# First FFN of an attention and two-FFN kernel: the next batch's scores ahead of its first two weight sets, and split sets and fetches in the first batch

## The chip, the cores and the metric

One core of a Trainium2 chip runs the whole kernel. Its engines are TensorE (PE in the profile, with PEld for the loading of weights), VectorE (DVE), ScalarE (ACT), GpSimd (POOL) and SyncE (SP). The metric is the device time of one execution in microseconds (us); lower is better. SP, ACT and POOL also issue transfers; the core's 16 DMA engines carry them out, and the profile shows the transfers of SP as queue q1, those of POOL as q0 and those of ACT as q10.

## The reference

```python
def _attn_ref(x, state):                      # x (8, 8, 512, 64), state (8, 8, 32, 64)
    scores = scale * np.matmul(x, state.transpose(0, 1, 3, 2))
    a = softmax(scores)
    xread = np.matmul(a, state)
    scores2 = scale * np.matmul(state, x.transpose(0, 1, 3, 2))
    a2 = softmax(scores2)
    sread = np.matmul(a2, x)
    return np.concatenate([xread, sread], axis=2)

def _moe_ref(x, w1, w2, w3, w_out):           # 4608 tokens, 512 -> 1024 -> 1024 -> 512
    h = (x @ w1) * (x @ w2) @ w3
    return h @ w_out

def _moe2_ref(x, w_gate, w_val, w_out):       # 512 -> 1536 -> 512
    return (sigmoid(x @ w_gate) * (x @ w_val)) @ w_out
```

`softmax` stands here for the lines that subtract the maximum, take the exponential and divide by the sum. The three stages run one after the other on the 4608 rows of the attention.

## The kernel before, in words

The kernel never forms the attention's `xread` for the first FFN. Since `xread @ w1` is `a @ (state @ w1)`, it makes for each of the 8 batches the small products of `state` with `w1` and `w2` and uses these as the weights of that batch. They come in four **sets** (quarters of the FFN's width). `StateWeights.fetch(q)` loads 1 MB of the converted `w1` and `w2` into one of two buffers `wq`; `StateWeights.make(q)` multiplies `state` with it on PE (results `psw`, two banks a set), and ACT and DVE split each bank into a high and a low part (`sw`). A `wq` buffer is free for the next fetch once PE has read it. So of the four fetches a batch needs, the third (quarter 2) can only be issued when `make(0)` is through PE, and the fourth when `make(1)` is.

The first FFN runs batch by batch (`t` from 0 to 7 in the loop at the end of the listing). In a batch `ffn1` has 12 places where other work is hung in, the **slots**: before each of the eight products `pab` (slots 0 to 7, `JF` is 8) and before each of the four output blocks `py` (slots 8 to 11). In these slots the kernel makes ready the next batch: `xt` in slots 6 and 7 turns its x (`pxt` to `xT`), `scores` and what follows in slot 8 computes both score products (`psc`) and the first half of the softmax, slot 9 the second half, slot 10 or 11 the sets 2 and 3. For `t` of 1 to 6 slot 8 held, in this order, `sread` (`psr`, the last reader of this batch's x), a piece of the conversion of the second FFN's weights (`todo`, which ends in stores `wd` and `wod` on POOL), `make(0, 1)`, the scores, and `get(2, 3)`, which fetches the quarters 2 and 3. In batch 0 everything is one slot later, and its sets 2 and 3 are in slot 11.

`load_x` loads the x of the batch after the next in eight transfers `xn` of 128 KB, one a head, each in rows of 64 numbers (256 bytes). Its buffer is free when `sread` has read the old x, so the eight wait for `psr`.

In this part of the kernel only PE's order is written out by hand. The order on ACT, DVE, POOL and SP is worked out at build time by the framework, from its own estimate of when an instruction could start, and is then fixed: an engine that waits for one instruction does not go on to the next.

Of the kernel before, what the change touches and what calls it, by code (L numbers as in the profile page):

```python
# [127 lines left out]
def tile_state_attention__then__gated_ffns(  # L128
# [31 lines left out]
    JF = DFF // P  # L160
# [112 lines left out]
    with tc.manual_schedule(engines={mybir.EngineType.PE}):  # L273
# [7 lines left out]
        def load_x(b):  # L281
            t = at.tile([P, G, SC, 2, D], F32, name="xn", bufs=2)
            xn[b] = t
            for h in range(H):
                nc.sync.dma_start(
                    out=t[:, h // 2, :, h % 2], in_=x[b, h].rearrange("(p c) d -> p c d", c=SC)
                )
# [236 lines left out]
        def behind(fn):  # L524
            with tc.issue_after(last["raw"].ins):
                fn()
# [470 lines left out]
        nxt = StateWeights(order[1])  # L997
# [76 lines left out]
        def open_wst():  # L1074
            p2["wst"] = tc.alloc_tile_pool(name="wst", bufs=1, reuse_waits="tile")
# [8 lines left out]
        def in_place(fn):  # L1084

            with tc.issue_after(p2["act"].ins), tc.issue_after(p2["dve"].ins):
                fn()
# [100 lines left out]
        for t, b in enumerate(order):  # L1188
            if t:
                cur, nxt = nxt, StateWeights(order[t + 1]) if t + 1 < B else DirectWeights()  # L1190
            slots = {i: [] for i in range(JF + KM)}
            if t == 0:
                slots[JF] += [after_wp, sreadt]
                after = {}
            for i, fns in after.items():
                slots[i] += fns
            if t == 1:
                open_wst()
            if t:
                for i in range(t == 1, JF + KM):  # L1200
                    if todo:
                        slots[i].append(lambda fn=todo.pop(0): in_place(fn))
            if t + 1 < B:
                go = lambda t=t: load_x(order[t + 1])
                if t:
                    slots[0].append((lambda go=go: behind(go)) if t < 2 else go)
                before, after = attention(order[t + 1])[:2] if t else (before1, after1)

                def get(*qs, nxt=nxt):
                    for q in qs:  # L1210
                        nxt.fetch(q)

                if t == 0:
                    slots[JF + 1].append(lambda nxt=nxt: nxt.make(0, 1))
                    slots[JF + 1].append(lambda get=get: get(2, 3))
                    for i, fns in before.items():
                        if i >= JF:
                            slots[i + 1] += fns
                    slots[JF + 3].append(lambda nxt=nxt: nxt.make(2, 3))
                else:  # L1220
                    slots[0].append(lambda get=get: get(0, 1))
                    for i, fns in before.items():
                        slots[i] += fns
                    slots[JF].insert(2, lambda nxt=nxt: nxt.make(0, 1))
                    slots[JF].append(lambda get=get: get(2, 3))
                    slots[JF + 2].append(lambda nxt=nxt: nxt.make(2, 3))
            else:
                slots[JF + 2].append(lambda nxt=nxt: nxt.weights(0))
            if t + 1 == B:
                slots[JF + 3].append(open_c1)  # L1230
            ffn1(t, S, 2, cur.weights, aT[b], slots, u0 if t == 0 else None)
# [3 lines left out]
        slots = {i: [] for i in range(JF + KM)}  # L1235
# [475 lines left out]
```

## Time and profile before

| | |
|---|---|
| median of 3 runs | 1285.46 us (1285.43 to 1286.4) |
| the profiled execution | 1287.98 us |
| its span, first to last instruction | 1286.2 us |
| PE busy | 1267.1 us, 99% of the span |
| DVE busy | 957.4 us, 74% |
| ACT busy | 669.1 us, 52% |
| granted TensorE clock | 0.998 of full speed |
| first FFN, batches 1 to 6 | from 132.0 to 448.5 us of the span |

The profile is of one execution, whose time lies 2.5 us above the median of the plain runs; sums made from its rows are differences, and are set on the median.

### The profile page before, as it was taken

Reading aid. Unit: us, or ns where it says so; the run is one execution under the profiler, and the core shown is the slowest. Engines: PE = TensorE matmul, PEld = TensorE weight load, DVE = VectorE, ACT = ScalarE, POOL = GpSimd, SP = SyncE. Lnnn points to the kernel's source line nnn. Section 1 sums busy time; section 2 is a strip of 40 time slices with the busy share of each in tenths; the row PEclk is TensorE's granted clock in tenths of the full one; section 3 lists DMA queues with packets and bytes.
Section 4 is the critical chain, followed back from the end, with each engine's and each line's share of the span. In section 5 each row is a group of like instructions: output and inputs, shape, how many; then the busy total and the mean of one; then the engine's idle time right before and its main releaser. Section 6 shows DMA issues by size and latency. Waiting matters only on the chain.

```text
span 1286.2 us, 21643 instructions
## 1 busy us (share of the span) xinstructions
PE 1267.1 (99%) x7868; PEld 1107.4 (86%) x7868; DVE 957.4 (74%) x1848; ACT 669.1 (52%) x1308; POOL 86.6 (7%) x162
## 2 busy tenths in 40 slices
PE   9999999999999999999999999999999999999996
PEld 8777877878878789988887888889999999999996
DVE  8996779788797856175959657687686868687666
ACT  8994757757677556352444343362345344434432
POOL 0000000000000000000000500004000300021000
PEclk9999999999999999999999999999999999999999
DMA  9886697896978722587765867668888888878853
GB/s 345 265 263 241 210 331 264 286 307 236 330 261 298 273 112 75 190 270 221 230 202 175 259 203 241 195 194 271 276 291 262 267 274 292 259 254 277 255 178 99
DMA packets 169121, 312.86 MB, mean 243 GB/s; under 512 B 45368, under 2 KB 63288, under 8 KB 162104
## 3 DMA queue, kind: packets, MB, share of 16 engines
q1 hardware_dynamic: 153492, 257.21, 62.3%
q0 software_dynamic: 9344, 44.57, 9.5%
q10 hardware_dynamic: 6180, 9.70, 2.2%
q8 instruction: 63, 1.03, 0.3%
q14 instruction: 42, 0.34, 0.1%
HBM read 256.38 MB, written 55.05 MB: 242 GB/s over the span
## 4 chain that ended last, share of the span: by engine, by line
PE 81%; DVE 9%; ACT 5%; DMA 3%; issue 1%; SPq 0%; ACTq 0%; POOL 0%; DVEq 0%; POOLq 0%
PE psA L1438 20%; PE po L1608 16%; PE psB L1438 10%; PE pab L235 9%; PE py L235 8%; PE pab L238 5%; PE psC L1438 4%; PE py L238 4%; DMA wq<-w12d 2%; PE psw L543 2%; DVE y L1168 1%; ACT r L207 1%; DVE p L1474 1%; DVE ph L1168 1%; PE pxt L300 1%
## 5 line engine op out<-in xcount | busy, mean ns | idle before, releaser
L1438 PE MATMUL psA<-y,wt 128*128 128x384 f32 (+1 forms) x1440 | 299.8, 356 | 0.0
L1438 PEld LDWEIGHTS psA<-y,wt 128*128 128x128 f32 x1440 | 259.0, 188 | 22.5
L1608 PE MATMUL po<-ph,wo 128*128 128x384 f32 (+1 forms) x1260 | 251.7, 358 | 5.7 <-ACT sv L168 3.3
L1608 PEld LDWEIGHTS po<-ph,wo 128*128 128x128 f32 x1260 | 225.1, 188 | 29.6 <-ACT sv L168 6.3
L168 ACT ACTIVATE u<-psA 128x384 f32<-128x384 f32 (+1 forms) x120 | 64.0, 533 | 228.0 <-PE psA L1438 213.7
L1438 PE MATMUL psB<-y,wt 128*128 128x384 f32 (+1 forms) x720 | 159.5, 356 | 0.0
L1438 PEld LDWEIGHTS psB<-y,wt 128*128 128x128 f32 x720 | 130.0, 188 | 11.2
L235 PE MATMUL pab<-aT,sw 128*128 128x512 f32 x512 | 139.4, 394 | 0.0
L235 PE MATMUL py<-u,wp 128*128 128x512 f32 (+1 forms) x576 | 131.9, 381 | 0.0
L235 PEld LDWEIGHTS py<-u,wp 128*128 128x128 f32 x576 | 102.8, 188 | 28.2 <-issue 8.3
L235 PEld LDWEIGHTS pab<-aT,sw 128*128 128x128 f32 x512 | 94.4, 188 | 19.2 <-DVE s L356 0.4
L1560 DVE TENSOR_TENSOR acc<-po,acc 128x384 f32<-128x384 f32 (+1 forms) x140 | 82.8, 605 | 31.3 <-PE po L1608 30.9
L1532 POOL DMA_DIRECT2D out<-sv x112 | 61.7, 551 | 600.1 <-DVE sv L1527 595.5
L1465 DVE TENSOR_TENSOR p<-psB,u 128x384 f32<-128x384 f32 (+1 forms) x60 | 36.6, 610 | 81.7 <-ACT u L168 68.9
L1467 ACT ACTIVATE p<-p 128x384 f32<-128x384 f32 (+1 forms) x90 | 50.7, 563 | 83.1 <-DVE p L1465 83.1
L1438 PE MATMUL psC<-y,wt 128*128 128x384 f32 (+1 forms) x360 | 79.8, 356 | 0.0
L238 PE MATMUL pab<-aT,sw 128*128 128x512 f32 x256 | 78.9, 390 | 0.0
L1168 DVE TENSOR_TENSOR ph<-p,ph 128x384 fp32r<-128x384 f32 (+1 forms) x120 | 70.2, 605 | 7.4 <-ACT ph L168 6.4
L1438 PEld LDWEIGHTS psC<-y,wt 128*128 128x128 f32 x360 | 65.0, 188 | 5.6
L238 PE MATMUL py<-u,wp 128*128 128x512 f32 (+1 forms) x288 | 67.7, 377 | 0.0
L168 ACT ACTIVATE ph<-p 128x384 fp32r<-128x384 f32 (+1 forms) x120 | 63.5, 564 | 0.2 <-DVE p L1168 0.2
L168 ACT ACTIVATE ph<-t 128x384 fp32r<-128x384 f32 (+1 forms) x90 | 49.4, 564 | 26.4 <-DVE t L1168 26.1
(142 smaller groups left out, 1836.6 us busy)
## 6 DMA issues: line engine op xcount, KB each, us to landing
wt<-wd SPq DMA_DIRECT2D x420, 256.0 KB, 3.5
wo<-wod SPq DMA_DIRECT2D x105, 512.0 KB, 3.7
wq<-w12d SPq DMA_DIRECT2D x32, 1024.0 KB, 8.7
raw<-in_moe_w SPq DMA_DIRECT2D x32, 512.0 KB, 6.8
wd<-wstb POOLq DMA_DIRECT2D x12, 1024.0 KB, 5.4
raw<-in_moe_w_out SPq DMA_DIRECT2D x20, 512.0 KB, 6.4
wd<-wsta POOLq DMA_DIRECT2D x12, 768.0 KB, 4.3
xn<-in_x SPq DMA_DIRECT2D x56, 128.0 KB, 7.1
```

Source lines behind the costliest of these rows:

```text
L168: return nc.scalar.activation(out=o, in_=i, func=AF.Copy)
L207: lambda: nc.scalar.activation(out=r16[:, :, 0], in_=lo, func=AF.Copy, scale=2.0**-29),
L235: nc.tensor.matmul(o, w[i], xx[k], start=begin and n == 0 and i + k == 0, stop=False)
L238: nc.tensor.matmul(o, w[1 - late], xx[late], start=False, stop=end and n == len(pairs) - 1)
L543: nc.tensor.matmul(pts[k][NS * g : NS * g + NS, a * WQ : (a + 1) * WQ], stT[64 * k : 64 * k + 64, g, self.b * NS : (self.b + 1) * NS], w[6 ...
L1168: nc.vector.tensor_tensor(out=o, in0=x0, in1=x1, op=ALU.subtract)
L1438: nc.tensor.matmul(o, w[:, i, kb * P : (kb + 1) * P], xx[kb][h], start=start, stop=i == 1 and kb == 1, skip_group_check=True,)
L1465: nc.vector.tensor_tensor(out=t, in0=o, in1=kept[a, what], op=ALU.add)
L1467: later(2, 0.0, lambda: nc.scalar.activation(out=t, in_=t, func=AF.Sigmoid))
L1532: nc.gpsimd.dma_start(out=dst[:, :, i * P : (i + 1) * P], in_=t[32 * i : 32 * i + 32].rearrange("t j d e -> t j (d e)"),)
L1560: nc.vector.tensor_tensor(out=acc[d, cc], in0=o, in1=acc[d, cc], op=ALU.add)
L1608: nc.tensor.matmul(o, w[:, jj, i, d * P : (d + 1) * P], x[h], start=k in (1, 6, 2) and jj == 0 and i + h == 0, stop=jj == 1 and i == 1, sk ...
```

## The change

For `t` of 1 to 6, `make(0, 1)` moves behind the scores in slot 8. In batch 0 the sets 0 and 1 are taken apart: `make(0)` and the fetch of quarter 2 stay in slot 9 ahead of the scores, `make(1)` and the fetch of quarter 3 go to slot 10.

```diff
                 if t == 0:
-                    slots[JF + 1].append(lambda nxt=nxt: nxt.make(0, 1))
-                    slots[JF + 1].append(lambda get=get: get(2, 3))
+                    slots[JF + 1].append(lambda nxt=nxt: nxt.make(0))
+                    slots[JF + 1].append(lambda get=get: get(2))
+                    slots[JF + 2].insert(0, lambda nxt=nxt: nxt.make(1))
+                    slots[JF + 2].insert(1, lambda get=get: get(3))
                     for i, fns in before.items():
                         if i >= JF:
                             slots[i + 1] += fns
@@ -1221,7 +1223,7 @@
                     slots[0].append(lambda get=get: get(0, 1))
                     for i, fns in before.items():
                         slots[i] += fns
-                    slots[JF].insert(2, lambda nxt=nxt: nxt.make(0, 1))
+                    slots[JF].append(lambda nxt=nxt: nxt.make(0, 1))
                     slots[JF].append(lambda get=get: get(2, 3))
                     slots[JF + 2].append(lambda nxt=nxt: nxt.make(2, 3))
```

On SP, in batch 1 (the same in batches 2 to 5), these are the transfers around slot 8; `w12d_59` and `w12d_60` are the quarters 2 and 3 of this batch, `xn` the loads of the x two batches on. Lines with - are the order before, with + the order after.

```order
 L181 DMA raw<-in_moe_w_gate 128x4x256 x2
 L181 DMA raw<-in_moe_w_val 128x4x256
-L285 DMA xn<-in_x 128x4x64 x3
+L285 DMA xn<-in_x 128x4x64 x5
 L519 DMA wq<-w12d_59 128x2048
 L519 DMA wq<-w12d_60 128x2048
-L285 DMA xn<-in_x 128x4x64 x5
+L285 DMA xn<-in_x 128x4x64 x3
 L181 DMA raw<-in_moe_w_val 128x4x256
```

Two of the eight `xn` loads have moved from behind the two fetches to ahead of them, although the diff names neither. Batch 6 has no `xn` loads.

On ACT, at the same place of batch 1, these are the evictions of the sets (`sw`), the exponentials of the scores (`e`, `st`), the eviction of the first output block (`ysb`) and, two rows on, its store; the numbers in names only tell instances apart.

```order
 L168 ACTIVATE u_1953<-asb 128x512
-L451 ACTIVATE sr<-psr,r_1498 128x64 x2
-L168 ACTIVATE sw_2017<-psw 128x512 x2
-L168 ACTIVATE sw_2041<-psw 128x512 x2
-L348 ACTIVATE e_2048,s_2050<-psc,m_2049 128x512 x2
+L451 ACTIVATE sr<-psr,r_1472 128x64 x2
+L168 ACTIVATE sw_2046<-psw 128x512 x2
+L348 ACTIVATE e_2000,s_2002<-psc,m_2001 128x512 x2
+L168 ACTIVATE sw_2070<-psw 128x512 x2
 L373 ACTIVATE st<-st 128x1024
 L168 ACTIVATE ysb<-py 128x512
```

The second set's evictions went behind the two exponentials; DVE's order changes likewise.

On PE, in batch 0, these are the two places where sets are made in slots 9 and 10, each behind a block `py`.

```order
 L238 MATMUL py<-u_1401,wp_81 128x512
 L238 MATMUL py<-u_1385,wp_81 128x512
-L543 MATMUL psw<-wq,stT 32x256 x32
+L543 MATMUL psw<-wq,stT 32x256 x16
 L323 MATMUL psc<-xT,stT 32x512 x8
 L235 MATMUL py<-u_1205,wp_80 128x512
@@ -326,4 +326,5 @@
 L238 MATMUL py<-u_1401,wp_81 128x512
 L238 MATMUL py<-u_1385,wp_81 128x512
+L543 MATMUL psw<-wq,stT 32x256 x16
 L235 MATMUL py<-u_1205,wp_80 128x512
 L235 MATMUL py<-u_1206,wp_80 128x512
```

Half of the 32 matmuls moved one output block on. In batches 1 to 6 PE's only difference is that `psw` and `psc` have changed places in slot 8.

## Rows read from the trace of the kernel before

**Rows 1.** The page: span, and PE's busy time, share and instructions.

```profile
span 1286.2 us, 21643 instructions
PE 1267.1 (99%) x7868; PEld 1107.4 (86%) x7868; DVE 957.4 (74%) x1848; ACT 669.1 (52%) x1308; POOL 86.6 (7%) x162
```

**Rows 2.** Windows of batches 1 to 5: length, busy time of engines, clock, DMA share.

```profile
132.02:185.03 53.01, 52.76 (x426) 42.03 (x425) 43.17 (x84) 35.49 (x67) 2.85 (x5) 1.00 0.77 267
185.03:238.05 53.02, 52.80 (x427) 42.09 (x426) 44.56 (x86) 36.28 (x69) 3.38 (x6) 1.00 0.79 269
238.05:290.80 52.75, 52.75 (x427) 42.11 (x426) 44.38 (x86) 36.31 (x69) 3.37 (x6) 1.00 0.87 301
290.80:343.50 52.70, 52.70 (x426) 42.01 (x426) 44.51 (x86) 36.29 (x69) 3.37 (x6) 1.00 0.81 281
343.50:396.00 52.50, 52.50 (x427) 42.10 (x426) 44.40 (x86) 36.56 (x69) 3.38 (x6) 1.00 0.84 288
```

**Rows 3.** Timeline of PE, batch 0, slot 9: start, length, work, idle time before it.

```profile
109.58 1.09 PE L543 MATMUL psw<-wq,stT 64*32 64x256 f32 x32
111.53 1.10 PE L543 MATMUL psw<-wq,stT 64*32 64x256 f32 x32 [0.85 <-DMA wq<-w12d]
112.42 1.07 PE L323 MATMUL psc<-xT,stT 64*32 64x512 f32 x16
113.41 3.92 PE L235 MATMUL py<-u,wp 128*128 128x512 f32 x16
118.99 3.79 PE L235 MATMUL py<-u,wp 128*128 128x512 f32 x16
```

**Rows 4.** Timeline of PE, batch 1: slot 8, then sets 2 and 3.

```profile
156.61 1.10 PE L438 MATMUL psr<-xn,a 128*32 128x64 f32 x64
157.64 1.96 PE L543 MATMUL psw<-wq,stT 64*32 64x256 f32 x64
...
171.60 1.09 PE L543 MATMUL psw<-wq,stT 64*32 64x256 f32 x32
172.95 1.10 PE L543 MATMUL psw<-wq,stT 64*32 64x256 f32 x32 [0.25 <-DMA wq<-w12d]
```

**Rows 5.** Timeline of SP's queue in batch 1.

```profile
157.77 3.09 SPq L285 DMA_DIRECT2D xn<-in_x  x3
160.96 2.29 SPq L519 DMA_DIRECT2D wq<-w12d  x2
163.30 9.25 SPq L285 DMA_DIRECT2D xn<-in_x  x5
```

**Rows 6.** Tile wq, SP's issues from 156 to 165 us and their landing.

```profile
L519 SPq DMA_DIRECT2D wq<-w12d x2: 632/1124/1617, 161.0 to 161.6; - x2
DMA to landing us min/median/max: 9.2/10.2/11.2
```

**Rows 7.** DMA from 166 to 170 us: packets, bytes, share of the engines.

```profile
DMA packets 249, 1.67 MB, mean 418 GB/s; under 512 B 47, under 2 KB 47, under 8 KB 47
q1 hardware_dynamic: 248, 1.65, 100.8%
```

**Rows 8.** DMA from 171 to 172 us.

```profile
DMA packets 913, 0.27 MB, mean 267 GB/s; under 512 B 904, under 2 KB 904, under 8 KB 909
q1 hardware_dynamic: 908, 0.26, 122.3%
```

**Rows 9.** DMA from 172 to 173 us, queue q10.

```profile
q10 hardware_dynamic: 113, 0.22, 67.7%
```

**Rows 10.** Timelines of DVE and ACT, batch 1, around the scores.

```profile
159.81 2.49 DVE L173 TENSOR_TENSOR sw<-psw,sw 128x512 fp32r<-128x512 f32 x4
...
167.18 1.06 ACT L373 ACTIVATE st<-st 128x1024 f32<-128x1024 f32 x1 [0.36 <-DVE st L370]
168.14 0.58 ACT L168 ACTIVATE ysb<-py 128x512 f32<-128x512 f32 x1
...
168.75 0.33 ACTq L1050 DMA_DIRECT2D yd<-ysb  x1
```

**Rows 11.** Batch 5: PE at sets 2 and 3; issue and landing of their fetches.

```profile
382.92 1.96 PE L543 MATMUL psw<-wq,stT 64*32 64x256 f32 x64
...
L519 SPq DMA_DIRECT2D wq<-w12d x2: 723/1002/1282, 372.3 to 373.0; - x2
DMA to landing us min/median/max: 8.7/9.6/10.5
```

**Rows 12.** Tile wq, SP's issues from 105 to 107, then 105 to 127 us: landing.

```profile
DMA to landing us min/median/max: 6.0/6.0/6.0
...
DMA to landing us min/median/max: 5.4/6.0/7.7
```

## The prediction

> **What bounds the kernel now.** The page comes first: PE is busy for 99% of the span [rows 1], so only two things can move the time, work added to PE or a wait of PE. The change adds no matmul and takes none away. It is therefore priced in waits of PE around the slots it touches, and the view for that is PE's timeline, where an idle stretch stands in brackets with its releaser.
>
> The windows by batch show how little there is to win. Batches 1 to 5 do the same work at full clock and take 53.01, 53.02, 52.75, 52.70 and 52.50 us [rows 2]. Taking the shortest as free of waits, the others hold 0.51 + 0.52 + 0.25 + 0.20 = 1.48 us of them. The timeline says where: in batch 1 the matmuls of set 3 wait for their fetch [rows 4]. Sets 2 and 3 would run in 1.89 us as sets 0 and 1 do; set 3 should start 0.95 us behind set 2, at 172.55, and starts at 172.95, so 0.40 of that batch's 0.51 lies here. In batch 5 the 64 matmuls run through without an idle mark [rows 11]. Its later fetch was issued at 373.05 and landed 10.5 us on, at 383.55 [rows 11], while PE wanted it at 382.92 + 0.95 = 383.87: a margin of 0.32 us. So in every one of these batches the fetch of quarter 3 lands just when it is needed, and its landing is what the change has to be asked about. In batch 0 the corresponding wait is for quarter 1, 0.85 us [rows 3].
>
> What sets that landing is seen in three views. SP issues three `xn`, then the two fetches, then five `xn` [rows 5]; the fetches land 9.2 and 11.2 us after issue [rows 6]. From 166 to 170 us queue q1 carries 1.65 MB in 248 packets and fills the engines at 100.8% [rows 7]: that is nearly the whole 2 MB of the two fetches. One microsecond later it carries 908 packets of 256 bytes [rows 8]: the `xn` issued behind them. The queue works its transfers off in the order of issue, and the engines are full, so whatever goes in ahead of the fetches delays them by its own transfer time.
>
> **The change, part by part.**
>
> *Batch 0, make(1) one slot on.* Set 0 runs at 109.58 and takes 0.95 us, the scores 0.99 us [rows 3], and an output block 5.58 us (113.41 to 118.99, [rows 3]). Set 1 then begins at 109.58 + 0.95 + 0.99 + 5.58 = 117.1, and its quarter has landed at 111.5. The wait goes: before, sets 0 and 1 took from 109.58 to 112.42, 2.84 us; without a wait 1.89. Gain 0.95 us. What is late next is quarter 3, fetched only when `make(1)` is through, at about 118.1. PE wants it after another block and set 2, at 118.05 + 5.58 + 0.95 = 124.6. The fetch issued alone at 105.5 landed in 6.0 us [rows 12]; so would this one, at 124.1, and the block covers it with 0.5 us to spare. If it took 7.7, the worst of this stretch [rows 12], 1.2 us would come back. I take nothing, since it too is issued alone.
>
> *Batches 1 to 6, scores ahead of sets 0 and 1.* On PE `psc` (1 us) and `psw` (1.89 us) change places: no time, and `psc` needs only banks and `xT` that are long ready. Quarter 2's buffer comes free 1 us later; SP does not feel it, since it is still issuing `xn` then: before, it reached the fetch at 160.96 [rows 5], 2.4 us after set 0 had run. On DVE the scores no longer stand behind four splits of 2.49 us [rows 10]; by the new order one split still goes before the subtraction and the exponential `st`, so the softmax ends about 1.5 us sooner. Nothing waits for that, it has a whole block of slack; the splits of sets 0 and 1 end later instead, at about 167.5, and PE needs their banks at 171.6. Both cost nothing.
>
> *What the scheduler made of it on SP* decides: in batches 1 to 5 two more `xn` are issued ahead of the fetches of quarters 2 and 3. That is 2 x 128 KB in rows of 256 bytes, 1024 packets. From below: at the 908 packets per us that q1 reached alone [rows 8] they take 1.13 us. From above: if issue and not transfer set the pace, 3.09 us for three [rows 5] makes 2.06 us for two. SP issues the fetches at 160.96 and their data flows from 166 on [rows 5, 7], so issue has some 4 us in hand; I take 1.2, near the transfer's row.
>
> The Trainium skill (DMA: Bandwidth & Descriptors, "Why small descriptors are slow (HBM only)") gives a 256-byte descriptor 11 cycles where 8 carry data. By that the 0.26 MB would take about 0.87 us at [rows 7]'s rate, as an estimate, and the sum below would come to some +4.8 us. The trace has 0.26 MB in a microsecond against 0.41 for large packets [rows 7, 8], a ratio of 0.63 and not 0.73; the row decides.
>
> *A second delay.* The first output block's store `yd` is issued at 168.75, behind `ysb`, which on ACT follows `st` [rows 10]; its packets run from 172 on and take 67.7% of the engines for a microsecond, 0.68 us [rows 9], just after the fetch's data. With `st` 1.5 us sooner the store comes at about 167.3, its packets about 170.5, and the fetch's tail now lasts until about 172: they meet. Between nothing and 0.68 us; I take half, 0.34.
>
> *Sum.* Quarter 3 lands 1.2 + 0.34 = 1.54 us later. Batches 1 to 4 have no margin: 4 x 1.54 = 6.16. Batch 5 has 0.32: 1.22. Batch 6 has no `xn`, nothing. Minus 0.95 in batch 0: **+6.4 us**. The profiled execution's 1287.98 us would become 1294.4. It lies 2.5 us above the median of the runs; on the median, 1285.46 + 6.4 = **1291.9 us**. With both terms at their low ends (1.13, 0): 4 x 1.13 + 0.81 - 0.95 = +4.4; with both high (2.74): 10.96 + 2.42 - 0.95 = +12.4. The likeliest's own range is 1289.9 to 1297.9 us.
>
> **The rivals.**
>
> *The fetches land as before* (not slower). The two `xn` fit into time in which the engines have room, or the landing is set by something else. For it: the later fetch lands only at 161.6 + 11.2 = 172.8 [rows 6], though from 171 on the queue carries hardly anything but small packets [rows 8]; a part of its landing is not transfer. Against it: the full engines of [rows 7]. Then only batch 0 counts: 1285.46 - 0.95 = 1284.5 us. From the first case it parts at a delay d with 4d + (d - 0.32) - 0.95 = 2.57 us, 0.2% of the time and about what a measurement here can tell from no change: d = 0.77 us. If the waits of batches 1 to 4 went too, which needs fetches that land sooner, it would be 1285.46 - 0.95 - 1.48 = 1283.0, still within 0.2%. So "faster" needs a gain that no row shows.
>
> *Issue becomes the bound.* Before, the five `xn` behind the fetches took 9.25 us to issue, 1.85 each [rows 5]: SP was held up. If the fourth and fifth are now held up ahead of the fetches, quarter 3 comes 2.06 us later or more, with the store 2.4: 9.6 + 2.08 - 0.95 = +10.7, 1296.2 us. For it: that row. Against it: after three `xn` and two fetches it was the sixth and later loads that were slow, so the queue takes five.
>
> *Batch 0 loses what it wins*: with a landing of 7.7 us 1.2 of the 0.95 us gained come back, a loss of 0.25, and the first case gives 1293.1 us. I give this 0.1, inside the first case's 0.58.
>
> **How the numbers follow.** First case, a delay above 1.1 us: 0.58. Issue-bound: 0.15. A delay between 0.77 and 1.1 us: 0.07. Less than 0.77, down to none: 0.17. All waits gone: 0.03. Slower by over 0.2% is the first three, 0.80; within 0.2% nearly all the rest; faster I put at 0.03. The range of 1286.0 to 1296.5 leaves out the lowest (no delay at all, 0.12, and all waits gone, 0.03) and the top of the issue-bound case (0.05).
>
> **What the profile after would show.** Right: SP's row reads five `xn`, two fetches, three `xn`; the set-3 matmuls wait some 1.9 us for `wq` in batches 1 to 4 and 1.2 in batch 5; batches 1 to 4 take 54 to 54.5 us; batch 0's wait is gone; batch 6 stays at 52.5. If the waits stand at 2.5 us and the fetches' issue has moved past 164 us in batch 1, issue was the bound. If the `yd` packets lie behind the fetch's data, the second delay was wrong. Prediction wrong: batches 1 to 4 unchanged in length, or a new wait of `py` or `pab` for splits or for `aT`.

## The result, and the profile after

The changed kernel takes 1293.73 us (median of six runs, 1292.94 to 1294.78) against 1285.93 for the kernel before (six runs, 1285.22 to 1287.9): a ratio of 1.0057, 95% interval 1.0046 to 1.0067, which is 5.9 to 8.6 us more (the two medians alone are 7.8 apart). The profiled execution took 1293.67 us, 5.7 more than that of before, with a span 5.5 us longer. The head of its page, beside [rows 1]:

```profile
span 1291.7 us, 21648 instructions
PE 1267.6 (98%) x7868; PEld 1107.5 (86%) x7868; DVE 957.7 (74%) x1848; ACT 669.6 (52%) x1308; POOL 86.6 (7%) x162
```

PE is busy for 0.5 us more than before; the other 5 us are waits. Batches 1 to 6 by windows, with the columns of [rows 2]:

```profile
131.45:185.75 54.30, 52.74 (x426) 42.05 (x425) 43.25 (x84) 35.53 (x67) 2.82 (x5) 1.00 0.76 265
185.75:240.25 54.50, 52.70 (x426) 42.05 (x425) 44.41 (x86) 36.49 (x69) 3.37 (x6) 1.00 0.79 275
240.25:294.32 54.07, 52.70 (x426) 42.05 (x425) 44.49 (x86) 36.38 (x69) 3.36 (x6) 1.00 0.81 278
294.32:348.46 54.14, 52.72 (x426) 42.05 (x425) 44.41 (x86) 36.49 (x69) 3.37 (x6) 1.00 0.80 277
348.46:401.59 53.13, 52.70 (x427) 42.05 (x425) 44.41 (x86) 36.50 (x69) 3.36 (x6) 1.00 0.81 279
401.59:454.05 52.46, 52.46 (x427) 42.16 (x425) 47.05 (x90) 35.89 (x69) 3.86 (x6) 1.00 0.71 266
```

The first five add up to 270.14 us against 263.98 in [rows 2], 6.16 more. The borders in [rows 2] lie up to 0.2 us behind the batches' starts; from `psr` of batch 1 to `psr` of batch 6 it is 263.79 us before and 270.10 after, 6.31 more. Batch 6, the only one of the six without `xn` loads, has no wait at all. PE's timeline of this kernel says where in a batch the time lies (first batch 0, then batches 1, 2, 3 and 5):

```profile
109.71 1.09 PE L543 MATMUL psw<-wq,stT 64*32 64x256 f32 x32
110.60 1.06 PE L323 MATMUL psc<-xT,stT 64*32 64x512 f32 x16
111.59 3.93 PE L235 MATMUL py<-u,wp 128*128 128x512 f32 x16
...
117.27 1.09 PE L543 MATMUL psw<-wq,stT 64*32 64x256 f32 x32
118.29 3.92 PE L235 MATMUL py<-u,wp 128*128 128x512 f32 x16
...
123.95 1.96 PE L543 MATMUL psw<-wq,stT 64*32 64x256 f32 x64
...
156.05 1.10 PE L438 MATMUL psr<-xn,a 128*32 128x64 f32 x64
...
171.04 1.09 PE L543 MATMUL psw<-wq,stT 64*32 64x256 f32 x32
173.69 1.10 PE L543 MATMUL psw<-wq,stT 64*32 64x256 f32 x32 [1.56 <-DVE xst L463]
174.72 0.50 PE L235 MATMUL py<-u,wp 128*128 128x512 f32 x1
...
225.31 1.09 PE L543 MATMUL psw<-wq,stT 64*32 64x256 f32 x32
228.21 1.10 PE L543 MATMUL psw<-wq,stT 64*32 64x256 f32 x32 [1.80 <-DMA wq<-w12d]
229.24 0.97 PE L235 MATMUL py<-u,wp 128*128 128x512 f32 x3
...
282.28 1.10 PE L543 MATMUL psw<-wq,stT 64*32 64x256 f32 x32 [1.37 <-DVE xst L463]
...
389.55 1.10 PE L543 MATMUL psw<-wq,stT 64*32 64x256 f32 x32 [0.43 <-DMA wq<-w12d]
```

In batch 0 no wait is left: set 0 at 109.71, set 1 a block later, sets 2 and 3 in one run. In batches 1 to 5 the second half of the last pair, set 3, waits. A figure used below is the **loss** of a batch: the time from set 2's start to the block behind set 3, above the 1.89 us that the two sets need. In batch 1 it is 174.72 - 171.04 - 1.89 = 1.79 us, in batch 2 it is 229.24 - 225.31 - 1.89 = 2.04.

Two releasers are named, the fetch (`wq`) and a copy on DVE (`xst`, line 463; in batches 1, 3 and 4). In batch 5 the same copy stands on DVE at this time:

```profile
390.09 0.28 DVE L463 COPY xst<-psrt 128x128 f32<-128x128 f32 x1
```

It ends at 390.37, after set 3 has started (389.55), so set 3 does not need it; that it ended just ahead of set 3 in three batches is a coincidence. The fetch fits to 0.1 us, also where the copy is named. Its issues in batches 1 and 2 with the landing in batch 2, then issue and landing in batch 3 (tile `wq`):

```profile
L519 SPq DMA_DIRECT2D wq<-w12d x2: 609/1405/2201, 161.7 to 164.0; - x2
...
L519 SPq DMA_DIRECT2D wq<-w12d x2: 610/1063/1516, 216.4 to 218.0; - x2
...
DMA to landing us min/median/max: 8.6/9.3/10.1
...
L519 SPq DMA_DIRECT2D wq<-w12d x2: 502/817/1132, 271.1 to 272.7; - x2
DMA to landing us min/median/max: 7.2/8.3/9.5
```

218.0 + 10.1 = 228.1 us, and set 3 starts at 228.21; in batch 3 272.7 + 9.5 = 282.2, and set 3, for which the copy is named, starts at 282.28. Batch 4 agrees (326.5 + 9.8 = 336.3, start 336.40); of batches 1 and 5 the trace has no landing. Ahead of the fetches SP has issued what the order foretold (batch 1, beside [rows 5]):

```profile
157.21 4.38 SPq L285 DMA_DIRECT2D xn<-in_x  x5
161.68 2.91 SPq L519 DMA_DIRECT2D wq<-w12d  x2
164.64 2.36 SPq L285 DMA_DIRECT2D xn<-in_x  x3
```

The prediction leaves out one thing that shares the engines with all of these. In the seven microseconds from 158 the engines mostly carry queue q0, POOL's two stores `wd` of converted weights (DMA of the kernel before, 158 to 165 us):

```profile
q0 software_dynamic: 283, 1.83, 78.1%
q1 hardware_dynamic: 863, 0.22, 13.7%
```

It goes with this that SP's fetches were issued some 4 us ahead of their data [rows 5, 7]. In the changed kernel the same stretch has 1.82 MB on q0 and 0.45 on q1. No run here moves the stores, so what they cost quarter 3 is not known.

### The profile page after: what moved, and what is told of

Same layout as the page of the kernel before. It is cut to its first block, busy times and chain, and to the rows that moved or that the text cites. A ratio compares the mean times of both kernels' runs of the same rounds, so it can differ in the third digit from the quotient of the medians.

```text
span 1291.7 us, 21648 instructions
## 1 busy us (share of the span) xinstructions
PE 1267.6 (98%) x7868; PEld 1107.5 (86%) x7868; DVE 957.7 (74%) x1848; ACT 669.6 (52%) x1308; POOL 86.6 (7%) x162
## 4 chain that ended last, share of the span: by engine, by line
PE 83%; DVE 11%; ACT 2%; DMA 1%; SPq 1%; issue 1%; ACTq 0%; POOL 0%; DVEq 0%; POOLq 0%
PE psA L1440 20%; PE po L1610 16%; PE pab L235 10%; PE psB L1440 10%; PE py L235 7%; PE pab L238 5%; PE psC L1440 4%; PE py L238 3%; PE pwp L235 2%; DMA wq<-w12d 1%; PE psw L543 1%; DVE y L1168 1%; DVE p L1476 1%; DVE ph L1168 1%; PE pwp L238 1%
```

## The experiments

Two theories. **A**: the loss is made on SP; the two `xn` loads ahead of the fetches of quarters 2 and 3 delay quarter 3 by their transfer. **B**: the loss comes from the new order of scores and sets on PE, DVE and ACT (splits later, softmax and store earlier, the `xst` copy), and the `xn` loads only go along. A third cost, the earlier store `yd`, can exist beside either.

The first edit sets SP's order by hand: in batches 1 to 5 exactly k of the eight `xn` loads are issued ahead of the two fetches, the rest behind. The other engines keep their order, instruction for instruction.

```diff
-                go = lambda t=t: load_x(order[t + 1])
+                def go(t=t):
+                    if t < 2:
+                        load_x(order[t + 1])
+                    else:
+                        with tc.issue_after(last["wq23"].ins):
+                            load_x(order[t + 1], range(k, H))
...
-                    slots[JF].append(lambda get=get: get(2, 3))
+                    def fetches(get=get, t=t):
+                        if t + 2 < B and k:
+                            load_x(order[t + 2], range(k))
+                            with tc.issue_after(last["xn"].ins):
+                                get(2, 3)
+                        else:
+                            get(2, 3)
+                        last["wq23"] = last["wq"]
+
+                    slots[JF].append(fetches)
```

**The changed kernel with k = 3**, SP's order of before.

> The changed kernel with only SP's order undone: in batches 1 to 5 three xn loads ahead of the fetches of quarters 2 and 3 and five behind, as before the change; PE, ACT, DVE and POOL keep the changed order. Theory A (the two loads moved ahead of the fetches delay quarter 3): the waits of set 3 fall back to those of before, 0.2 to 0.4 us a batch, plus at most 0.34 us for the earlier store; time between 1 us below and 1 us above before. Theory B (the new order on ACT and DVE keeps PE waiting: the profile names DVE's copy xst as releaser in three of the five waits): the waits of 1.4 to 1.9 us stay, time about 7.5 us above before.

1286.7 us, ratio to the kernel before 1.0001 (0.9992 to 1.001). The loss is gone; batch 2 on PE:

```profile
223.05 1.09 PE L544 MATMUL psw<-wq,stT 64*32 64x256 f32 x32
224.42 1.10 PE L544 MATMUL psw<-wq,stT 64*32 64x256 f32 x32 [0.28 <-DMA wq<-w12d]
```

All that the diff reorders on PE, DVE and ACT is still there, and the time is that of before: against B.

**The kernel before with k = 5**, SP's order of the change and nothing else of it.

> The kernel before with only SP's order changed: five xn loads ahead of the two fetches in batches 1 to 5; all other engines in the order of before. Theory A: set 3 waits some 1.2 us longer in batches 1 to 4 and 0.9 in batch 5, time 5.5 to 8.5 us above before (the upper end if the store had no part in the delay). Theory B: time as before, within 1 us.

1294.74 us, ratio 1.0063 (1.0051 to 1.0076). SP's order alone makes the whole loss, without the new order of scores and sets; its size in the trace goes above A's in batch 3, where the clock fell (last section).

**The changed kernel with k = 0.** All eight loads go behind the fetches.

> The changed kernel with all eight xn loads behind the two fetches in batches 1 to 5. Theory A: quarter 3 lands some 3 us sooner than in the changed kernel, no wait for it is left in any batch, time 2.4 us below before (0.95 of batch 0, 1.48 of the waits that stood before). Theory B: time about 7.5 us above before. A third way: the loads now come so late that the next batch's transposes of x or the raw loads behind them wait; then slower than before again, with waits of pxt or of the conversion.

1284.44 us, ratio 0.9984 (0.9975 to 0.9993): faster than both kernels. No set waits in batches 1 to 6, which last 52.46 to 52.48 us. But its batch 0 does wait:

```profile
123.60 1.09 PE L544 MATMUL psw<-wq,stT 64*32 64x256 f32 x32
126.03 1.10 PE L544 MATMUL psw<-wq,stT 64*32 64x256 f32 x32 [1.33 <-DMA wq<-w12d]
127.06 1.20 PE L235 MATMUL py<-u,wp 128*128 128x512 f32 x4
```

127.06 - 123.60 - 1.89 = 1.57 us, more than what was won there. Its quarter 3 was issued at 118.1 and took 7.8 us to land, in the changed kernel 5.2 (tile `wq` on SP from 115 to 120 us, of this kernel):

```profile
L520 SPq DMA_DIRECT2D wq<-w12d x1: 319/319/319, 118.1 to 118.1; - x1
...
DMA to landing us min/median/max: 7.8/7.8/7.8
```

**The kernel before with k = 0**, the gain of the moved loads without the change.

> The kernel before with all eight xn loads behind the two fetches in batches 1 to 5, nothing else changed. Theory A: the waits that stood before (1.4 to 1.5 us over batches 1 to 4) go, every batch takes 52.5 us, time 1.4 us below before; the order of scores and sets is worth nothing by itself, so this is within 0.5 us of the changed kernel with the same loads, up to batch 0. If the scores in front have a worth of their own, this one stays above it by that.

1285.21 us, ratio 0.9991 (0.9983 to 1.0). Batches 1 to 5 last 52.47 to 52.48 us, as with the changed order: in these batches the order of scores and sets by itself is worth nothing.

**The changed kernel with k = 8**, to have a dose.

> The changed kernel with all eight xn loads ahead of the two fetches in batches 1 to 5. If every load ahead costs its transfer (between three and five loads the waits of five batches grew by 5.9 us, 0.59 us a load), three more add 3 x 0.59 = 1.8 us in each of five batches: waits of about 3.4 us, time about 9 us above the changed kernel, 16 above before. If what counted was that SP's issue is pushed past some point, the step from five to eight is much larger (SP needs up to 2 us a load once it is held up: 6 us a batch, 30 us in all) or, if the queue has room, much smaller.

1311.67 us, ratio 1.02 (1.0184 to 1.0217). In batch 1 SP is at the fetches 10.8 us after the batch's `psr`, in the changed kernel 5.6 us:

```profile
156.35 9.57 SPq L286 DMA_DIRECT2D xn<-in_x  x8
166.02 1.04 SPq L520 DMA_DIRECT2D wq<-w12d  x2
```

The issue has moved by 5.2 us for three loads. Quarter 3's landing moved far less: set 3 starts 19.4 us after `psr` at 155.19, against 17.6 in the changed kernel, so 1.8 us for three, 0.6 each. With three loads it is 16.4, with none the fetch lands after 14.6. The step from three loads to five goes by transfer and not by issue: the second fetch is issued 5.0 us after `psr` in the kernel before and 7.9 in the changed one, 2.9 later, and set 3 starts 1.3 later. With eight loads this can't be told: the fetches land 5.9 and 7.8 us after issue, and a pair issued at 124.3 and 125.2 us of the same trace, with no `xn` ahead of it, took 5.4 and 7.6 (both of tile `wq` on SP).

```profile
DMA to landing us min/median/max: 5.9/6.8/7.8
...
DMA to landing us min/median/max: 5.4/6.5/7.6
```

So there issue may be what sets the landing. The windows of batches 1 to 3, here from `psr` to `psr`, show what is new:

```profile
155.19:211.19 56.00, 52.77 (x427) 42.15 (x426) 44.90 (x88) 36.59 (x70) 3.34 (x6) 1.00 0.76 268
211.19:271.06 59.87, 55.57 (x426) 43.76 (x425) 44.53 (x87) 36.60 (x70) 3.37 (x6) 0.94 0.74 251
271.06:326.50 55.44, 52.78 (x427) 42.16 (x426) 44.61 (x87) 36.51 (x70) 3.36 (x6) 1.00 0.79 271
```

Set 2 now waits too, and batches 1 and 3 lose 3.5 and 3.0 us over 52.48; in batch 2 (and batch 5) the clock falls as well and takes more. With those the dose is not one of transfer alone, so its total (25 us above before, where 16 was expected) says nothing on the price of a load.

**Batch 0's part alone** and **the part of batches 1 to 6 alone**: one half of the diff each.

> Only the batch 0 part of the change. Both theories: the wait of 0.85 us for quarter 1 goes, quarter 3 is covered, time 0.95 us below before. If quarter 3 now lands late, time 0 to 0.4 us above before.

> Only the part of the change for batches 1 to 6; batch 0 as before. Theory A: the full loss without what batch 0 gave, 7.4 us above before plus what batch 0 was worth: 0.95 us if quarter 3 lands in time there, nothing or less than nothing if it lands late as in the run with all loads behind. So 7 to 8.5 us above before.

1286.08 us, ratio 0.9998 (0.9989 to 1.0007), and 1295.16 us, ratio 1.0068 (1.0052 to 1.0083). The loss lies in batches 1 to 6. Batch 0's gain is not seen in the times, though the interval reaches to -1.4 us and holds the 0.95 forecast. In the trace of batch 0's part quarter 3 of batch 0 took 6.5 us to land and PE lost 0.26 us on it.

**The store behind the second output block.** In the changed kernel, batches 1 to 6, the first block's `yd` is held and issued together with the second's; k is left at 5.

```diff
-                for i, at_, of, w in pieces:
-                    nc.scalar.dma_start(out=y_d[i][d, :, at_ : at_ + w], in_=ysb[:, of : of + w])
+
+                def put(ysb=ysb, d=d):
+                    for i, at_, of, w in pieces:
+                        nc.scalar.dma_start(out=y_d[i][d, :, at_ : at_ + w], in_=ysb[:, of : of + w])
+
+                held.append(put)
+                if d or c not in range(1, 7):
+                    while held:
+                        with tc.issue_after(p2["act"].ins):
+                            held.pop(0)()
```

> The changed kernel with the store of the first output block issued behind the eviction of the second block, in batches 1 to 6 (some 5 us later), so that its packets can't meet the fetches. If the early store is part of the delay (the second delay of the prediction, 0.34 us a batch), the waits shrink by that and the time falls by 1.5 us, at most 3.4 (0.68 a batch). If it is not, the time is that of the changed kernel, 7.4 us above before.

1291.72 us, ratio 1.0041 (1.0029 to 1.0054), where the changed kernel has 1.0057 (1.0046 to 1.0067): 2 us less, but the intervals overlap. The losses of batches 1 to 5 add up to 6.76 us, 1.01 less than in the changed kernel: 0.2 a batch. Two things weaken this run. The table below has 7.77 and 8.53 us for two traces with the same order in these batches, so 1.01 is hardly more than traces differ by. And the build moved more than the store: on DVE some splits of sets (`sw`) change places too.

The run does tell something of issue. In batch 1 SP comes later to the fetches than in the changed kernel (second issue at 164.0 there, 165.2 here; `psr` at 156.05 and 155.86), and set 3 does not start later, at 173.37, 17.5 us after `psr` against 17.6.

**Set 3 of batch 0 in slot 0 of batch 1**, first on the kernel before with batch 0's part, then on the changed kernel with k = 0, so that the slow landing is covered.

```diff
-                    slots[JF + 3].append(lambda nxt=nxt: nxt.make(2, 3))
+                    slots[JF + 3].append(lambda nxt=nxt: nxt.make(2))
                 else:
+                    if t == 1:
+                        slots[0].append(lambda cur=cur: cur.make(3))
                     slots[0].append(lambda get=get: get(0, 1))
```

> The kernel before with only batch 0 changed: set 1 one slot on, as in the change, and set 3 one block further on, in slot 0 of batch 1. If quarter 3's landing (5.2 to 7.8 us in four runs) is what took batch 0's gain away in part of the executions, the gain is now steady: 0.95 us below before. If batch 0's gain was lost elsewhere, the time is that of before.

> The changed kernel with all eight xn loads behind the two fetches in batches 1 to 5, and with batch 0's set 3 made one block later, in slot 0 of batch 1, so that its fetch has 5.6 us more. If both waits are what the earlier runs showed, no set waits for its quarter in any batch: 0.95 us of batch 0 and 1.4 of batches 1 to 4, time 2.4 us below before. If the late set 3 makes batch 1 wait (its products need the banks of set 3, and the fetches for the next batch come a block later), 1 us or more of it is lost, and batch 1 is longer than 52.5 us plus the 0.95 us of the set moved into it.

1286.71 us, ratio 1.0002 (0.9993 to 1.0011), and 1284.66 us, ratio 0.9987 (0.9978 to 0.9996). No set waits in batch 0 in either trace. The second beats both kernels, but by 1.7 us and not by the 2.4 expected, no more than k = 0 alone does; the wait taken from batch 0 shows in neither time.

The losses of the traces, in us, worked out as above from each kernel's timeline of PE (the run with k = 8 left out, since its set 2 waits too). Three rows are repeats: the two halves of the diff have in batches 1 to 5 the instruction order of the kernel named with them, and batch 0's set 3 late has it behind slot 0 of batch 1.

| kernel | 1 | 2 | 3 | 4 | 5 | sum |
|---|---|---|---|---|---|---|
| before (3 loads ahead) | 0.49 | 0.45 | 0.20 | 0.22 | 0 | 1.36 |
| batch 0's part, as before (3) | 0.25 | 0.42 | 0.37 | 0.34 | 0 | 1.38 |
| batch 0's set 3 late, as before (3) | 0.06 | 0.03 | 0.08 | 0.18 | 0 | 0.35 |
| changed (5) | 1.79 | 2.04 | 1.61 | 1.66 | 0.67 | 7.77 |
| batches 1 to 6, as changed (5) | 1.78 | 1.86 | 2.07 | 1.81 | 1.01 | 8.53 |
| changed, 3 | 0.50 | 0.51 | 0.32 | 0.38 | 0.18 | 1.89 |
| changed, 5, store late | 1.65 | 1.39 | 1.65 | 1.20 | 0.87 | 6.76 |
| before, 5 | 1.49 | 2.04 | 3.02 | 1.40 | 1.29 | 9.24 |
| either, 0 | 0 | 0 | 0 | 0 | 0 | 0 |

So one and the same order can differ by about 1 us between two traces.

## Why the prediction was right

**The main term, two more `xn` ahead of the fetches.** Shown, by the pair of runs that make the loss without the change and take it away with it. Forecast 1.2 us a batch. Between the changed kernel with 5 and with 3 loads ahead lie 7.77 - 1.89 = 5.88 us, 1.18 a batch as a mean: 1.3 to 1.5 in batches 1 to 4 and 0.5 in batch 5. That is 0.59 us a load. With the store's part in it, changed less before is 6.41 us or 0.64 a load, and in the repeat from the two halves (8.53 - 1.38) / 10 = 0.72. Set 3's idle marks are 1.37 to 1.80 us in batches 1 to 4, where the text had some 1.9. The measured 1.18 goes with the 908 packets a microsecond of [rows 8]. That row holds 904 small packets and 4 of 8 KB, so the small ones alone carry 0.23 MB in the microsecond, and their ratio to [rows 7] is 0.56 and not the 0.63 of the text. The Trainium skill's 11 cycles for 8 (DMA: Bandwidth & Descriptors, "Why small descriptors are slow (HBM only)") led to an estimate of about 0.87 us for two; the traces lie above it.

**The rival of issue** is out, although its sign in part came: one of the two fetches was held up in issue, and the second went out at 164.0 us in batch 1, 2.4 us later than before, where the text had named 164. But set 3 did not wait the 2.5 us that went with it, and where the store is late the second fetch went out at 165.2 with no longer wait of set 3. With eight loads issue may well be the bound; with five it is not.

**The rival of no delay** is out: the delay d was above 0.77 in batches 1 to 4.

**The second delay, the store**, is not settled. It was issued at 166.94 us instead of 168.75 (forecast 167.3), and its packets (queue q10) meet the fetch's (q1) in the microsecond from 170, where [rows 9] had them from 172:

```profile
q1 hardware_dynamic: 45, 0.33, 79.2%
q10 hardware_dynamic: 27, 0.06, 14.3%
```

Most of them come in the next microsecond, 112 packets, where q1 has nearly only small packets, the loads behind the fetch. So they meet, as forecast, but only in part. Forecast 0.34 us a batch; taking it away gives back 0.20 a batch in the losses, and with SP's order as before the new order costs (1.89 - 1.36) / 5 = 0.11. Both are within what traces of one order differ by, so whether the term was too large, and whether it is there at all, stays open.

**Batch 5** was forecast at 1.22 us and lost 0.67 (1.01 in the repeat): with its margin of 0.32, quarter 3 came 1.0 to 1.3 us later there and not 1.54. **Batches 1 to 4** were forecast at 54 to 54.5 us and took 54.07 to 54.50; **batch 6** at 52.5, took 52.46. **Edits costed at nothing** cost nothing: with no load ahead both orders run through at 52.46 to 52.48 us a batch.

**Batch 0's gain of 0.95** is 0.70 in the trace of the changed kernel. No wait is left, but from `psr` of batch 0 to `psr` of batch 1 it takes 156.05 - 75.84 = 80.21 us, where the kernel before takes 156.61 - 75.71 = 80.90. The text counted an output block as 5.58 us; the two blocks beside the single set take 117.27 - 111.59 = 5.68 and 123.95 - 118.29 = 5.66, where in the kernel before two blocks in a row took 11.11 (from 113.41 to set 2 at 124.52). With set 3 made later as well it is 80.53, so 0.37 of the gain is left, too little for these times to show.

The step that is not sure is the landing of quarter 3, taken as 6.0 us with 0.5 to spare. Of the six traces that have it in this place it took 5.0 to 5.3 us in four, then 6.5 and 7.8. With 7.8, in the changed kernel with k = 0, batch 0 takes 81.73 us, 0.8 more than before. The rival of a loss there thus came about in one trace of the six.

**The sum.** By the trace: losses 7.77 - 1.36 = 6.41, less 0.70, +5.7 us; the span grew by 5.5. With the two halves, which have the same orders, it is 8.53 - 1.38 - 0.70 = +6.5. Forecast +6.4, and the times say +5.9 to +8.6. The mechanism and its size are right to about 1 us; that +6.4 lies so near is not proof of each term, since the store is open and batch 0 gave less than forecast. The profiled execution of before lay 2 us above its median and that of after on it, which is most of the gap between 5.5 and 7.3; what took those 2 us in the one execution is not known.

## What to carry over

Where PE is full, ask what stands ahead of each due transfer on its queue, and let the order of issue after the edit answer, since a scheduler may hoist loads that the diff doesn't name. Here loads that nobody waited for were better behind the fetches that somebody did: the same edit is 0.6% slower than the kernel before with five loads ahead, the same with three and 0.16% faster with none. When a named releaser changes from batch to batch while the wait doesn't, look for the one event that fits all of them.

## Not expected of the hardware

Not every wait costs only its length. In the kernel before with k = 5, batch 3, set 3 waits and then takes 1.96 us (PE's timeline; the same 32 matmuls take 1.10 us elsewhere), and the windows have the granted clock at 0.50, the lower of the two levels (1.2 GHz), until about 286 us:

```profile
282.56 1.96 PE L544 MATMUL psw<-wq,stT 64*32 64x256 f32 x32 [1.93 <-DMA wq<-w12d]
```

```profile
282.00:284.00 2.00, 1.44 (x32) 0.87 (x32) 1.75 (x3) 1.81 (x4) 0.00 (x0) 0.66 1.18 320
284.00:286.00 2.00, 2.00 (x19) 1.26 (x5) 2.00 (x5) 1.08 (x2) 0.00 (x0) 0.50 1.10 421
286.00:288.00 2.00, 2.00 (x10) 1.66 (x9) 1.92 (x5) 0.00 (x0) 0.00 (x0) 0.99 1.04 431
```

That batch is 56.21 us long where batch 2, whose set 3 waits 1.80 us at full clock, has 54.52. In the run with k = 8 it happens with two waits in a row, of 2.12 and 2.18 us in batch 2; the clock falls within the second (mean 0.73 from 230 to 232 us, then 0.50 to 236). PE's timeline:

```profile
228.37 1.10 PE L544 MATMUL psw<-wq,stT 64*32 64x256 f32 x32 [2.12 <-DVE aT L173]
231.65 1.96 PE L544 MATMUL psw<-wq,stT 64*32 64x256 f32 x32 [2.18 <-DMA wq<-w12d]
233.54 5.86 PE L235 MATMUL py<-u,wp 128*128 128x512 f32 x16
```

The block `py` behind them takes 5.86 us for 16 matmuls that take 3.92 in [rows 3]. In batch 1 of that run, with waits of 1.83 and 1.40 us, the window's clock is 1.00. The length of the waits alone does not tell when it happens: in batch 4, with 1.44 and 1.84 us, the clock stayed at 1.00, and in batch 5, with 1.02 and 1.65 us, it fell: the second 32 matmuls took 1.85 us there. The prediction had no term for this. The changed kernel, with waits up to 1.80 us, stayed clear of it in the profiled execution.
